# Filler matmuls ahead of an output projection, two equal evictions, and an early sqrt table in a one-core decode kernel

## The chip, the cores and the metric

The kernel runs on one core of one Trainium2 chip. The metric is the device time of one execution in microseconds; lower is better. Executions agree to a few tenths of a microsecond, so 2% (3.7 us) is far outside the noise. Where a profile is read, times are counted from the start of its span, which is about 1.3 us shorter than the time of the run. In the views PE is TensorE (matrix multiplication), PEld its loading of the stationary operand, ACT is ScalarE, DVE VectorE, POOL GpSimd, and SP is SyncE, whose queue issues the loads. The granted clock is the share of its full speed at which TensorE was allowed to run.

## The reference, cut to what matters

One decode step of an adaptive-LayerNorm block: two rows of 640 numbers, 32 heads of 192, a window of 1024 cached keys and values per head, a gated feed-forward part of 1536 hidden units.

```python
mod = (_silu(c) @ w_mod).reshape(c.shape[0], 6, 1, -1)      # sa, ca, ga, sb, cb, gb
h = _layernorm(x) * (1 + ca) + sa
# A: attention over the last 1024 cached positions, then @ wo   (6144 x 640)
x = x + ga * A(h)
h = _layernorm(x) * (1 + cb) + sb                            # "LN2"
# B: (gelu(h @ w_gate) * (h @ w_up)) @ w_down                  (640 x 1536, 1536 x 640)
x = x + gb * B(h)
```

With two rows there is hardly any arithmetic per byte: 76.9 MB of weights and cache are read once for one small result. The weights are loaded in this order, in one queue: w_mod, wq, the cache tiles, wo (two parts), w_gate, w_up, w_down (three parts).

## The kernel before

After attention, everything hangs on one chain: `sel` (gathers the attention result), wo, the row sums of wo, the residual, LN2, gate, up, the product, its transposition, down, the residual, the store. The parts that the change touches:

```python
S.op("pe", p_sel, ...)                                        # sel
S.op("act", ... activation(out=oT, in_=ps[:, BK_OT, ...], func=Copy), name="oT")
NA = D - QW                                                   # 640 = 512 + 128
for ci, (t0, n) in enumerate(WO_SPLIT):                       # 39 tiles, then 9
    ...
    for bk, lo, w in ((2, 0, QW), (3, QW, NA)):               # one matmul of 512, one of 128
        last = e.matmul(ps[32*i:32*i+B, bk, 0:w], lhsT=oT[:, t, :], rhs=wv[:, tl, lo:lo+w],
                        ..., tile_position=(0, 32*i))         # i = t % 4: four column strips
S.op("act", ... activation(out=wS[:, 0:QW], in_=ps[:, 2, :], func=Copy), name="wo_evac0")
S.op("dve", ... tensor_copy(out=wS[:, QW:D], in_=ps[:, 3, 0:NA]), name="wo_evac1")
# [cut: row sums, residual]
def ln_stats(tag):
    ...                                                       # act: Square with row sum; dve: sum; pe: both
    S.op("dve", ... tensor_copy(out=mv, in_=ps[:, BK_M, CS:CS+2]))           # mean, mean of squares
    S.op("dve", ... nvar = mean*mean - meansq)
    S.op("dve", ... nvar = -nvar + EPS)
    S.op("act", ... activation(out=st2[:, 0:1], in_=nvar, func=Sqrt))        # a table load stands in front
    S.op("dve", ... reciprocal(out=rstd, in_=st2[:, 0:1]))
def ln_mod(...):
    S.op("dve", ... lnt = (X - mean) * (1 + scale))
    S.op("dve", ... hrow = lnt * rstd + shift)
# [cut: transposition of hrow to h2T]
def ffn_gu(...):                                              # gate, then up
    wk = wv[:, k, :].rearrange("p (m i r) -> p i m r", i=NR, r=FR)   # strip i reads 3 of every 12 elements
    for i in range(NR):
        e.matmul(ps[32*i:32*i+B, bk, 0:FT], lhsT=h2T[:, k, :], rhs=wk[:, i, :, :], tile_position=(0, 32*i))
```

## Time and profile before

| | |
|---|---|
| time, median of the first 3 runs | 186.26 us (186.07 to 186.29) |
| span of the profiled run | 184.8 us |
| DMA busy, mean of 16 engines | 97% in the load queue |
| read from memory | 76.88 MB, 416 GB/s over the span |
| granted TensorE clock, mean | 0.878 |

From the page of the kernel before: three of the rows that cut the span into 40 slices (granted clock and DMA share in tenths), and the line on memory. The clock falls in several places. The DMA share stays at 7 tenths or more in every slice but the last.

```profile
PEclk9999999999999669997569999978999559975858
DMA  9999998999798989999898989999998989899980
...
HBM read 76.88 MB, written 0.00 MB: 416 GB/s over the span
```

The chain of work that ended last, in order of time (start us, us, what), of the kernel before, cut to the pieces that matter. After wo has landed at 164.57 it waits for no DMA: it runs through wo (6.31), a table load (1.28), gate and up (3.66), down (1.04).

```profile
137.63 26.94 DMA arena<-in_A_wo_dram
...
164.61 6.31 PE ps L629 x96
...
173.29 1.28 ACT L421
...
174.58 0.21 ACT st L421
...
176.38 3.66 PE ps L663 x34
...
181.28 1.04 PE ps L691 x48
```

The windows of the kernel before (stretch, its length, busy time of PE, PEld, DVE, ACT and POOL with instruction counts, granted clock, DMA share, GB/s). In the first stretch PE is busy for 1.38 of 3.40 us; in the two after it, which hold wo, the clock is at 0.50.

```profile
160.20:163.60 3.40, 1.38 (x20) 0.71 (x14) 0.19 (x1) 0.86 (x2) 0.00 (x0) 1.00 0.88 367
163.60:167.00 3.40, 2.39 (x36) 0.67 (x20) 0.00 (x0) 0.00 (x0) 0.00 (x0) 0.50 1.02 433
167.00:170.40 3.40, 3.40 (x56) 0.93 (x28) 0.00 (x0) 0.00 (x0) 0.00 (x0) 0.50 1.01 428
```

Last, the load stream beside that chain. First the loads' issue times on SyncE's queue (timeline), then the list of DMA issues (KB each, us from issue to landing), both of the kernel before.

```profile
155.90 0.33 SPq L285 DMA_DIRECT2D arena<-in_B_w_up_dram  x1
156.27 1.40 SPq L285 DMA_DIRECT2D arena<-in_B_w_down_dram  x3
```

```profile
arena<-in_B_w_up_dram SPq DMA_DIRECT2D x1, 1920.0 KB, 21.3
...
arena<-in_B_w_down_dram SPq DMA_DIRECT2D x1, 1280.0 KB, 24.0
arena<-in_B_w_down_dram SPq DMA_DIRECT2D x1, 480.0 KB, 24.7
arena<-in_B_w_down_dram SPq DMA_DIRECT2D x1, 160.0 KB, 24.6
```

Issue plus time to landing gives 177.2 us for w_up and 180.3, about 181.5 and 181.9 for the parts of w_down (the three issues lie about 0.47 us apart).

### The profile page before, as it was taken

Reading aid. Unit: us, or ns where it says so; the run is one execution under the profiler, and the core shown is the slowest. Engines: PE = TensorE matmul, PEld = TensorE weight load, DVE = VectorE, ACT = ScalarE, POOL = GpSimd, SP = SyncE. Lnnn points to the kernel's source line nnn. Section 1 sums busy time; section 2 is a strip of 40 time slices with the busy share of each in tenths; the row PEclk is TensorE's granted clock in tenths of the full one; section 3 lists DMA queues with packets and bytes.
Section 4 is the critical chain, followed back from the end, with each engine's and each line's share of the span. In section 5 each row is a group of like instructions: output and inputs, shape, how many; then the busy total and the mean of one; then the engine's idle time right before and its main releaser. Section 6 shows DMA issues by size and latency. Waiting matters only on the chain.

```text
span 184.8 us, 1589 instructions
## 1 busy us (share of the span) xinstructions
PE 104.6 (57%) x826; PEld 28.5 (15%) x549; DVE 106.7 (58%) x99; ACT 14.5 (8%) x27; POOL 6.5 (4%) x27
## 2 busy tenths in 40 slices
PE   0016300956665095653599565947663299849182
PEld 0012000120000000002360001600000256512042
DVE  6214000039994499964992999587995547600502
ACT  2032100041000000001000000010000100100720
POOL 7600000000000000000000000000000000000000
PEclk9999999999999669997569999978999559975858
DMA  9999998999798989999898989999998989899980
GB/s 333 466 479 426 426 426 362 440 426 505 346 511 362 489 383 468 457 394 502 351 493 351 500 362 489 404 447 426 436 482 362 502 357 508 357 395 432 422 361 26
DMA packets 2626, 76.97 MB, mean 417 GB/s; under 512 B 314, under 2 KB 444, under 8 KB 572
## 3 DMA queue, kind: packets, MB, share of 16 engines
q1 hardware_dynamic: 2604, 76.88, 97.0%
q8 instruction: 5, 0.08, 0.2%
q14 instruction: 1, 0.01, 0.0%
q10 hardware_dynamic: 16, 0.01, 0.0%
HBM read 76.88 MB, written 0.00 MB: 416 GB/s over the span
## 4 chain that ended last, share of the span: by engine, by line
DMA 57%; DVE 20%; PE 19%; ACT 2%; issue 1%; DVEq 0%
DMA arena<-in_A_k_cache_dram 35%; DMA arena<-in_A_wo_dram 15%; DVE arena L506 11%; DMA arena<-in_w_mod_dram 7%; PE ps L518 5%; DVE S_sb L525 4%; PE ps L569 4%; PE ps L629 3%; PE ps L458 2%; PE ps L663 2%; DVE Em L555 1%; ACT L421 1%; PE ps L691 1%; DVE hrow L430 0%; PE ps L439 0%
## 5 line engine op out<-in xcount | busy, mean ns | idle before, releaser
L518 PE MATMUL ps<-arena,ident_b 128*128 128x512 bf16 x192 | 49.1, 399 | 29.0 <-DVE arena L506 29.0
L506 DVE TENSOR_TENSOR arena<-arena,qbc 128x3072 bf16<-128x3072 bf16 x32 | 54.8, 1753 | 9.8 <-DMA arena<-in_A_k_cache_dram 9.8
L569 PE MATMUL ps<-arena,Em 128*64 128x384 bf16 x256 | 26.9, 381 | 5.6 <-DVE Em L555 5.6
L525 DVE TENSOR_REDUCE S_sb<-ps 128x32 f32<-128x1024 f32 x16 | 19.5, 1222 | 8.2 <-PE ps L518 8.2
L569 PEld LDWEIGHTS ps<-arena,Em 128*64 128x64 bf16 x256 | 16.6, 129 | 31.0 <-DVE Em L555 22.0
L555 DVE TENSOR_TENSOR Em<-E_sb,maskE 128x2048 bf16<-128x2048 bf16 x8 | 18.0, 2285 | 3.8 <-PE ps L569 3.8
L480 PE MATMUL ps<-arena,hT 128*2 128x512 bf16 x60 | 6.0, 587 | 11.8 <-DMA arena<-in_A_wq_dram 11.8
L490 DVE CAST qrow<-ps 128x512 bf16<-128x512 f32 x1 | 0.7, 692 | 17.0 <-PE ps L480 17.0
L533 PEld LDWEIGHTS ps<-ident_f,M 128*1 128x1 f32 x2 | 0.2, 79 | 60.9 <-DVE M L531 60.9
L629 PE MATMUL ps<-arena,oT 128*2 128x512 bf16 (+1 forms) x96 | 6.3, 454 | 2.4 <-DMA arena<-in_A_wo_dram 2.4
L637 DVE COPY arena<-ps 128x128 f32<-128x128 f32 x1 | 0.3, 293 | 10.6 <-PE ps L629 10.6
L543 ACT ACTIVATE E_sb<-S_sb,nbias 128x256 bf16<-128x256 f32 x2 | 1.0, 507 | 67.0 <-DVE nbias L541 67.0
L576 ACT ACTIVATE On<-ps,rden 128x384 bf16<-128x384 f32 x2 | 1.2, 580 | 49.9 <-PE ps L569 49.9
L399 PE MATMUL ps<-ident_b,crow 2*128 2x2 bf16 x5 | 0.4, 177 | 7.9 <-DMA crow<-in_c_dram 7.9
L458 PE MATMUL ps<-arena,scT 128*17 128x480 bf16 x40 | 4.3, 597 | 0.3 <-DMA arena<-in_w_mod_dram 0.3
L412 PE MATMUL ps<-st,selstat 128*128 128x2 f32 x4 | 0.9, 298 | 6.1 <-ACT sqj L408 6.1
L404 DVE CAST X<-xr 128x160 f32<-128x160 bf16 x1 | 0.2, 243 | 6.4 <-DMA xr<-in_A_x_dram 6.4
L663 PE MATMUL ps<-arena,h2T 128*2 128x384 bf16 x40 | 3.6, 507 | 0.3 <-DVE h2T L443 0.3
L480 PEld LDWEIGHTS ps<-arena,hT 128*2 128x2 bf16 x20 | 0.7, 118 | 16.8 <-issue 16.8
L466 DVE TENSOR_SCALAR opc<-modR 128x160 f32<-128x160 f32 x2 | 0.5, 244 | 4.3 <-ACT modR L463 4.3
L439 PE MATMUL ps<-selrow,hrow 128*32 128x2 bf16 x40 | 0.7, 182 | 3.8 <-DVE hrow L430 3.8
L672 DVE TENSOR_TENSOR aR<-ps,gl 128x384 bf16<-128x384 f32 x1 | 0.6, 557 | 3.8 <-PE ps L663 3.8
(84 smaller groups left out, 52.7 us busy)
## 6 DMA issues: line engine op xcount, KB each, us to landing
arena<-in_A_v_cache_dram SPq DMA_DIRECT2D x4, 6144.0 KB, 26.7
arena<-in_A_k_cache_dram SPq DMA_DIRECT2D x3, 6144.0 KB, 36.9
arena<-in_A_wq_dram SPq DMA_DIRECT2D x1, 7680.0 KB, 31.1
arena<-in_A_wo_dram SPq DMA_DIRECT2D x1, 6240.0 KB, 26.9
arena<-in_A_k_cache_dram SPq DMA_DIRECT2D x2, 3072.0 KB, 42.9
arena<-in_w_mod_dram SPq DMA_DIRECT2D x1, 4800.0 KB, 13.8
arena<-in_B_w_gate_dram SPq DMA_DIRECT2D x1, 1920.0 KB, 19.5
arena<-in_B_w_up_dram SPq DMA_DIRECT2D x1, 1920.0 KB, 21.3
```

Of the source, the lines that this page charges most:

```text
L421: S.op("act", lambda e: e.activation(out=st2[:, 0:1], in_=nvar[:, :], func=ACTF.Sqrt), reads=["nvar"], writes=[("st2", 0)], name=tag + "_s ...
L458: last = e.matmul(ps[32 * i:32 * i + RM, half, 0:MH].rearrange("p (m n) -> p m n", n=DR), lhsT=scT[:, k, :], rhs=wv[:, 3 * half:3 * half + ...
L480: last = e.matmul(ps[32 * i:32 * i + B, n, :], lhsT=hT[:, k, :], rhs=wv[:, kk, i, n * QW:(n + 1) * QW], start=(k == 0), stop=(k == KT - 1) ...
L506: S.op("dve", lambda e: e.tensor_tensor(out=kt, in0=kt, in1=qbc[:, b, :].unsqueeze(1).broadcast_to([P, JC, Dh]), op=ALU.mult), reads=[("qb ...
L518: last = e.matmul(o_ap, lhsT=ident_b[:, :], rhs=kt[:, :, t * GC:(t + 1) * GC], start=(t == 0), stop=(t == NCH - 1))
L525: S.op("dve", lambda e: e.tensor_reduce(out=S_sb[:, b, 2 * JC * pair:2 * JC * (pair + 1)], in_=ps[:, 2 * z:2 * z + 2, :].rearrange("p k (j ...
L555: S.op("dve", lambda e, z=z, j=j: e.tensor_tensor(out=Em[:, z, :, :], in0=E_sb[:, b, j:j + JE].unsqueeze(2).broadcast_to([P, JE, H]), in1= ...
L569: last = e.matmul(ps[64 * i:64 * i + 2 * H, BK_O, 0:ON], lhsT=Em[:, z, 2 * jp:2 * jp + 2, :].rearrange("p j h -> p (j h)"), rhs=view(it, l ...
L576: S.op("act", lambda e: e.activation(out=On[:, b, :], in_=ps[:, BK_O, 0:ON], func=ACTF.Identity, scale=rden[:, b:b + 1]), reads=[bank(BK_O ...
L629: last = e.matmul(ps[32 * i:32 * i + B, bk, 0:w], lhsT=oT[:, t, :], rhs=wv[:, tl, lo:lo + w], start=(t < NR), stop=(t >= NT - NR), tile_po ...
L663: last = e.matmul(ps[32 * i:32 * i + B, bk, 0:FT].rearrange("p (m r) -> p m r", r=FR), lhsT=h2T[:, k, :], rhs=wk[:, i, :, :], start=(k == ...
L691: last = e.matmul(ps[32 * i:32 * i + RM, BK_OT, CY:CY + DR], lhsT=aT[:, fc, :], rhs=wv[:, i, :], start=(fc == WD_SPLIT[0][0]), stop=(fc == ...
```

## The change

Its intent is to shorten the chain after attention: keep PE busy while it waits for wo, so that wo, which ran at a granted clock of 0.50 before, runs at full clock (`clock0`), and again around LN2 (`clock1`, `clock2`); evict wo's sums in two halves of equal length; load the sqrt table while PE waits for wo; drop the separate variance operation by adding EPS where the mean is copied and letting sqrt scale by -1; and compute the scaled difference while sqrt runs.

```diff
+        def keep_clock(n, name):      # n matmuls of 128x512, result never read
+            ... e.matmul(ps[:, BK_T, :], lhsT=ident_b, rhs=Em[:, 0, ...], start=True, stop=True)
         def ln_stats(tag):
+            if tag == "ln2":
+                keep_clock(5, "clock2")
-            S.op("dve", ... tensor_copy(out=mv, in_=ps[:, BK_M, CS:CS + 2]))
+            S.op("dve", ... tensor_tensor(out=mv, in0=ps[:, BK_M, CS:CS + 2], in1=epsc, op=add))
-            S.op("dve", ... tensor_scalar(out=nvar, in0=nvar, scalar1=-1.0, scalar2=EPS, ...))
-            S.op("act", ... activation(out=st2[:, 0:1], in_=nvar, func=Sqrt))
-            S.op("dve", ... reciprocal(out=rstd, in_=st2[:, 0:1]))
+            S.op("act", ... activation(out=st2[:, 0:1], in_=nvar, func=Sqrt, scale=-1.0))
         def ln_mod(...):
             S.op("dve", ... lnt = (X - mean) * (1 + scale))
+            S.op("dve", ... reciprocal(out=rstd, in_=st2[:, 0:1]))
 [cut]
         S.op("pe", p_sel, ...)
+        keep_clock(9, "clock0")
         S.op("act", ... name="oT")
+        S.op("act", ... activation(out=junk, in_=epsc[:, 0:1], func=Sqrt), name="sqrt_table")
-        NA = D - QW
+        NA = D // 2
-                    for bk, lo, w in ((2, 0, QW), (3, QW, NA)):
+                    for bk, lo, w in ((2, 0, NA), (3, NA, NA)):
 [cut: wo_evac0 and wo_evac1 with NA columns each]
         S.op("pe", wo_rows, ...)
+        keep_clock(5, "clock1")
```

## The prediction

> **What bounds the kernel now.** The page gives the DMA queues 97% of 16 engines over the span of 184.8 us, at 416 GB/s; the weight stream never pauses. The list of DMA issues, with its time to landing, puts the last arrivals (estimates: issue plus time to landing) at: first part of wo 164.6 us, second part 168.0, w_gate 172.6, w_up 177.2, the three parts of w_down 180.3, 181.5 and 181.9. The chain of waits says instead that the tail is compute: from wo's landing at 164.57 it runs through wo, LN2, gate/up, down without waiting for DMA. Both are nearly true: down's 48 matmuls run 181.28 to 182.32, and the last of them need bytes that land at 181.9. So the compute chain has only about 0.1 to 0.3 us over the DMA stream.
>
> **What the change does, step by step.**
> - Fillers. The windows show the granted clock falling to 0.50 at 163.6 us, so all of wo (6.27 us, groups of eight matmuls every 0.53 us) ran at half clock.[...] Nine 512-column fillers (about 0.22 us each warm, 0.43 cold: estimates from half and full-clock columns of wo) fit in the 2.36 us for which PE waits for wo. At full clock wo0 would end about 167.2, then wait for the second part (168.0) and end about 168.7 instead of 170.92: 2.2 us.
> - Halves. The ScalarE eviction of 512 columns took 0.60 us; 320 should take about 0.45 on each engine. 0.15 us.
> - Sqrt. The table load took 1.28 us[...] and held sqrt until 174.58, when its input had been ready at 174.41. With one small DVE operation gone (0.15) and the scaled difference (0.37 busy) behind the sqrt, 0.7 to 0.8 us.
> - The later fillers (five each) fit into PE idle of 1.3 us if warm; if cold they cost up to 0.8 us.
>
> Added up: 3 us of chain, h2T at about 173.2 instead of 176.34. Then the DMA takes it back. Gate may start at 173.2, but up cannot start before w_up lands at 177.2; it was at 178.3 before. The intermediate is ready about 179.5, down0 waits until 180.3, down1 until 181.5, the last four matmuls until 181.9. They take 0.24 us warm[...]; down ends near 182.15 to 182.25 against 182.32. The last 2.5 us (two DVE operations and the store) are unchanged. The diff moves no large load, and their issues all hang on earlier stages.
>
> **Predicted time.** 186.1 us (before: 186.26), range 185.6 to 186.5. Faster by over 2%: 1%; within 2%: 98%; slower: 1%.
>
> **What would show it.** wo's group spacing 0.27 us, no idle before wo beyond the landing, PE then waiting for the second part of wo; only one table load between wo and gelu; new waits of up and down on the DMA of w_up and w_down; the chain ending in DMA of w_down; last landings unmoved within 0.2 us.
>
> **What would make it wrong.** If the last landings move: the tail of the stream is uneven[...]. Or if the fillers run cold and late enough to use up the 3 us of slack, which I doubt.

That fillers keep the clock up was then the author's assumption; with them wo ran at 1.00 in the profile after. 2.2, 0.15 and 0.7 to 0.8 us come to the 3 us. One figure behind down's end is cut, the time of its last four matmuls at the lower clock. With the 0.24 us (down's matmuls took 233 ns on average in the profile before) 181.9 gives about 182.15; the way up to 182.25 is allowance. That the end of the stream is uneven shows in the profile before: the DMA share drops from 9 to 4 tenths at about 179.5 us and stays at 2 or 3 tenths until about 181.3.

## The result, and the profile after

| | before | after |
|---|---|---|
| time, median (6 runs each) | 186.05 us (185.89 to 186.29) | 185.97 us (185.91 to 186.12) |
| ratio | | 0.9996, 95% interval 0.9983 to 1.0009 |
| span of the profiled run | 184.8 us | 184.9 us |
| mean granted clock, profiled run | 0.878 | 0.926 |

A ratio is the mean time of one kernel's runs over that of the other's of the same rounds, so it is not quite the ratio of the medians quoted. The result is "same": nothing that the noise lets one see.

The slices of the profile after: the clock is full from the 34th slice on. The DMA row looks as before.

```profile
PEclk9999999996999759998599999987999669999999
```

The timeline of the profile after (start us, us, engine, line, operation; in brackets the idle time before and what ended it):

```profile
161.13 1.89 PE L415 MATMUL ps<-Em,ident_b 128*128 128x512 bf16 x8
161.41 1.28 ACT L632 ACT_TABLE_LOAD   x1
...
164.80 2.89 PE L643 MATMUL ps<-arena,oT 128*2 128x320 bf16 x78 [1.78 <-DMA arena<-in_A_wo_dram]
...
168.27 0.98 PE L643 MATMUL ps<-arena,oT 128*2 128x320 bf16 x18 [0.58 <-DMA arena<-in_A_wo_dram]
...
172.58 0.20 ACT L433 ACTIVATE st<-nvar 128x1 f32<-128x1 f32 x1 [0.98 <-DVE nvar L430]
...
174.09 1.91 PE L678 MATMUL ps<-arena,h2T 128*2 128x384 bf16 x20 [0.27 <-DVE h2T L455]
...
177.45 1.91 PE L678 MATMUL ps<-arena,h2T 128*2 128x384 bf16 x20 [1.45 <-DMA arena<-in_B_w_up_dram]
...
181.70 0.64 PE L706 MATMUL ps<-arena,aT 128*17 128x160 bf16 x16 [0.31 <-DMA arena<-in_B_w_down_dram]
182.09 0.10 PEld L706 LDWEIGHTS ps<-arena,aT 128*17 128x17 bf16 x4 [0.21 <-DMA arena<-in_B_w_down_dram]
```

The fillers ahead of wo and the LN2 part did what they were meant to. wo ran at full clock, waited for its second part, and was done at 169.25 in place of 170.92. Sqrt started at 172.58 in place of 174.58. Gate started at 174.09 in place of 176.38, 2.3 us earlier. Then the new waits begin: up stands 1.45 us until w_up has landed, and both later parts of down wait for w_down. Down ended where it had ended before (182.37, before 182.32). The chain of the profile after says it shortest: it no longer holds wo or LN2 but reaches from w_down's load to the end.

```profile
155.58 26.07 DMA arena<-in_B_w_down_dram
181.65 0.04 issue
181.70 0.39 PE ps L706 x12
182.08 0.01 issue
182.09 0.28 PE ps L706 x4
182.37 0.02 issue
182.39 0.34 DVE fin L711
```

### The profile page after: what moved, and what is told of

It reads as the page before. It is cut to its first block, busy times and chain, and to the rows that moved or that the text cites. A ratio compares the mean times of both kernels' runs of the same rounds, so it can differ in the third digit from the quotient of the medians.

```text
span 184.9 us, 1610 instructions
## 1 busy us (share of the span) xinstructions
PE 104.3 (56%) x843; PEld 26.1 (14%) x552; DVE 106.8 (58%) x97; ACT 14.5 (8%) x28; POOL 6.7 (4%) x29
## 4 chain that ended last, share of the span: by engine, by line
DMA 57%; DVE 22%; PE 17%; ACT 1%; issue 1%; SPq 0%
DMA arena<-in_A_k_cache_dram 36%; DMA arena<-in_B_w_down_dram 14%; DVE arena L518 12%; DMA arena<-in_w_mod_dram 8%; PE ps L581 8%; DVE S_sb L537 6%; PE ps L530 5%; DVE Em L567 2%; PE ps L470 2%; DVE negm L547 1%; ACT E_sb L555 1%; PE ps L558 1%; DVE M L543 0%; PE ps L551 0%; SPq L287 0%
## 5 line engine op out<-in xcount | busy, mean ns | idle before, releaser
L530 PE MATMUL ps<-arena,ident_b 128*128 128x512 bf16 x192 | 50.7, 411 | 30.2 <-DVE arena L518 30.1
L581 PE MATMUL ps<-arena,Em 128*64 128x384 bf16 x256 | 24.5, 357 | 5.6 <-DVE Em L567 5.6
L581 PEld LDWEIGHTS ps<-arena,Em 128*64 128x64 bf16 x256 | 15.4, 121 | 29.8 <-DVE Em L567 22.2
L492 PE MATMUL ps<-arena,hT 128*2 128x512 bf16 x60 | 4.7, 485 | 11.7 <-DMA arena<-in_A_wq_dram 11.7
L651 DVE COPY arena<-ps 128x320 f32<-128x320 f32 x1 | 0.5, 491 | 10.1 <-PE ps L643 10.1
L643 PE MATMUL ps<-arena,oT 128*2 128x320 bf16 x96 | 3.9, 299 | 2.4 <-DMA arena<-in_A_wo_dram 2.4
L415 PE MATMUL ps<-Em,ident_b 128*128 128x512 bf16 x17 | 4.2, 379 | 0.2 <-issue 0.2
```

Source lines behind the costliest of these rows:

```text
L415: last = e.matmul(ps[:, BK_T, :], lhsT=ident_b[:, :], rhs=Em[:, 0, 0:512 // H, :].rearrange("p j h -> p (j h)"), start=True, stop=True)
L492: last = e.matmul(ps[32 * i:32 * i + B, n, :], lhsT=hT[:, k, :], rhs=wv[:, kk, i, n * QW:(n + 1) * QW], start=(k == 0), stop=(k == KT - 1) ...
L530: last = e.matmul(o_ap, lhsT=ident_b[:, :], rhs=kt[:, :, t * GC:(t + 1) * GC], start=(t == 0), stop=(t == NCH - 1))
L581: last = e.matmul(ps[64 * i:64 * i + 2 * H, BK_O, 0:ON], lhsT=Em[:, z, 2 * jp:2 * jp + 2, :].rearrange("p j h -> p (j h)"), rhs=view(it, l ...
L643: last = e.matmul(ps[32 * i:32 * i + B, bk, 0:w], lhsT=oT[:, t, :], rhs=wv[:, tl, lo:lo + w], start=(t < NR), stop=(t >= NT - NR), tile_po ...
```

## The experiments

**Theory.** The stream of loads ends at the same time in both kernels, and its end bounds both; the chain got about 2 us shorter and now waits. **Rivals**: (A) the stream alone matters and the chain was far from it in both kernels; (B) the chain never got shorter in sum, since the fillers and the table load cost what they gave. Twelve kernels were run, each in 5 rounds on one of three chips; the kernel before ran beside them, with medians of 186.00, 186.02 and 185.99 us. To see the chain at all one has to take the end of the stream away, so most of them load only one fifth of w_up, which makes w_down land about 3.7 us earlier (an estimate; its middle part landed at 177.9 us in place of 181.65). Their outputs are wrong, which doesn't matter for the times. The instructions on the compute engines stay the same.

### 1. The end of the stream taken away, kernel before

```diff
-    S.dma("sp", k_dma(view(it), source(it)), ...)
+    cut = F if it[0] == "wu" else place[it][1]           # w_up: 1536 of 7680 elements per partition
+    S.dma("sp", k_dma(view(it, 0, cut), source(it)[:, 0:cut] ...), ...)
```

> The kernel before, with only one fifth of w_up loaded (wrong result on purpose), so that everything loaded after it lands about 3.7 us earlier (1.57 MB at 416 GB/s). Theory (two nearly equal bounds: compute chain just ahead of the DMA stream in the kernel before): no gain, 0 to 0.3 us, because the compute chain from wo on stays. Rival A (the DMA stream alone bounds both kernels): 3 us or more faster. Rival B (the change never shortened the chain): no gain here and none in the changed kernel either.

Measured: median 185.12 us (184.63 to 185.88, 6 runs) against 186.00, ratio 0.9951 (0.9933 to 0.9970). This is 0.9 us, more than the 0 to 0.3 expected, and far less than rival A's 3 us. The six runs spread over 1.25 us, where the kernel before spread over 0.4. So in most runs the compute chain of the kernel before was already shorter than the stream, by up to 1.4 us, and the end of the stream hid how much it varied. The one profile that I had read, of a run at 186.16 us, was a long one. Its wo ran 6.31 us; in the profile of this experiment wo took 5.65: the step between its groups of eight matmuls fell from 0.53 to 0.27 us at about 169 us, where in the profile before the granted clock rose from 0.50 to 1.00 only at 170.4.

```profile
164.67 5.65 PE ps L631 x96
...
180.67 1.04 PE ps L693 x48
```

### 2. The same for the changed kernel

The edit is that of experiment 1, in the changed kernel.

> The changed kernel with the same cut load (wrong result on purpose). Theory: with up no longer waiting for w_up the chain shows its true gain: down ends about 2.1 us earlier than in the changed kernel, so about 183.8 to 184.0 us, 2.0 to 2.3 us under the kernel before. Rival A (DMA alone): 3 us or more faster, as much as the kernel before gains from the same cut. Rival B (the change's fillers and loads cost what they gave): about 186.0, no gain.

Measured: median 183.61 us (183.50 to 183.79, 4 runs), ratio 0.9870 (0.9857 to 0.9883). This is a little under the expected 183.8 to 184.0. Both rivals fall: the chain is shorter by 1.5 us between the medians of the two cut kernels (185.12 and 183.61), yet the gain is not what a stream alone would give. In its chain down starts at 178.87, in place of 180.67 above, without a wait for w_down.

```profile
173.94 3.69 PE ps L680 x22
...
178.87 1.04 PE ps L708 x48
```

### 3. The stream made longer, both kernels

Here 393 KB more are loaded between w_up and w_down into a free part of the arena; nobody reads them and the results are right.

```diff
+    place[("pad", 0)] = (o_d + FC * D, 13 * HS - o_d - FC * D)     # 1536 elements per partition
 [cut]
+    if kind == "pad":
+        return B_w_up.rearrange("(p k) n -> p (k n)", k=KT)[:, 0:place[it][1]]
```

> The kernel before with 393 KB more to load between w_up and w_down (0.95 us of stream at 416 GB/s; nobody reads it, the result stays right). Theory: the stream had about 0.1 to 0.25 us to spare, so 0.7 to 0.9 us slower. Rival B, compute alone: under 0.2 us slower.

> The changed kernel with the same 393 KB more to load. Theory: it already waits for the last bytes of w_down, so the whole 0.95 us shows (0.85 to 1.05 us slower than the changed kernel), about 186.95. Rival B, compute alone: under 0.2 us slower.

Measured: before 186.94 us (186.87 to 187.03), ratio 1.0049 (1.0037 to 1.0061); after 187.00 (186.92 to 187.09), ratio 1.0052 to the kernel before (1.0040 to 1.0064). The changed kernel lost 1.03 us (187.00 against its 185.97 of other rounds), as expected. The kernel before lost 0.94, a shade more than the 0.7 to 0.9 expected: it loses all of the 0.95 us, so it too waits for the stream in most runs. Together with experiment 1 this settles what bounds the two kernels. In the profile of the kernel before with the longer stream, down waits for w_down where it did not before:

```profile
181.43 0.73 PE L694 MATMUL ps<-arena,aT 128*17 128x160 bf16 x32 [0.56 <-DMA arena<-in_B_w_down_dram]
```

### 4. Which part of the change shortened the chain

Four kernels with the cut load, each with one part of the change taken out. The edits: all three `keep_clock` calls removed; only `clock1` and `clock2` removed; `NA = D - QW` and its evictions put back; the LN2 operations put back and `sqrt_table` removed.

> Changed kernel, cut w_up load, without any filler matmuls (halves and sqrt part kept). Theory (fillers give the wo stage, and what they give depends on where the run's 3.4 us clock windows fall): 0.9 to 1.8 us slower than the changed kernel with the cut load (183.61), so 184.5 to 185.4, and the runs spread by about 1 us again as those of the kernel before with the cut load did (184.63 to 185.88), not by 0.3. Rival C (fillers are worth nothing, gain is sqrt alone): within 0.2 us of 183.6.

> Changed kernel, cut w_up load, with the nine fillers ahead of wo alone, the five and five around LN2 taken out. Theory (gate and up ran at 0.35 us a group at full clock as at half, so the clock there is worth nothing): within 0.15 us of 183.61. Rival D (later fillers keep gate and up fast): 0.5 us or more slower.

> Changed kernel, cut w_up load, wo sums split 512/128 as before. Trace: from the end of wo to the start of its row sums 0.67 us in the kernel before, 0.66 in the changed one. Theory from that: within 0.1 us of 183.61. My recorded prediction gave this step 0.15 us.

> Changed kernel, cut w_up load, LN2 as before (table load in front of sqrt, separate variance operation, scaled difference after the sqrt). Trace: from the statistics matmul to the start of the last LN2 operation 1.89 us before, 1.28 changed. Theory: 0.6 us slower than 183.61, about 184.2. My recorded prediction gave this step 0.7 to 0.8.

| cut load, changed kernel | median us | range | ratio to before |
|---|---|---|---|
| whole change | 183.61 | 183.50 to 183.79 | 0.9870 |
| no fillers | 184.98 | 184.29 to 185.52 | 0.9941 |
| only the nine ahead of wo | 183.65 | 183.36 to 184.53 | 0.9866 |
| halves undone | 183.79 | 183.61 to 184.50 | 0.9888 |
| LN2 part undone | 184.68 | 184.04 to 185.26 | 0.9928 |

All fillers together are worth 1.4 us between medians, as expected (the nine ahead of wo alone 1.3: 184.98 against 183.65), and without them the spread of 1.2 us is back. The ten later ones are worth 0.04. The halves are worth 0.2 between medians, more than the 0.1 expected. But the profiled run of that kernel, its slowest at 184.50, shows another cause: the nine fillers ended at 162.64, PE then stood for 2.1 us, and wo ran at half clock for a time (5.11 us). Timeline and windows of that profile:

```profile
160.53 2.11 PE L417 MATMUL ps<-Em,ident_b 128*128 128x512 bf16 x9
164.76 5.11 PE L645 MATMUL ps<-arena,oT 128*2 128x512 bf16 x96 [2.12 <-DMA arena<-in_A_wo_dram]
170.58 0.47 PE L659 MATMUL ps<-arena,selw 128*17 128x160 f32 x8 [0.71 <-ACT arena L651]
...
172.41 0.35 PE L426 MATMUL ps<-st,selstat 128*128 128x2 f32 x2 [0.17 <-ACT sqj L422]
...
174.12 0.37 PE L453 MATMUL ps<-selrow,hrow 128*32 128x2 bf16 x20 [0.26 <-DVE hrow L444]
```

```profile
161.80:165.20 3.40, 1.28 (x16) 0.19 (x8) 0.00 (x0) 0.71 (x2) 0.00 (x0) 0.99 0.92 385
165.20:168.60 3.40, 3.40 (x58) 1.02 (x28) 0.00 (x0) 0.00 (x0) 0.00 (x0) 0.50 1.03 438
```

The same 5.11 us of wo stand in the profiled runs of the kernels with nine fillers alone (its slowest, 184.53) and with the LN2 part undone (its slowest, 185.26). So the nine fillers hold the clock in some runs and not in others. This goes with where the clock's windows of 3.41 us happen to lie: in the profile of the changed kernel the window from 161.27 still held 1.75 us of busy PE and the clock stayed full; in the fence above the window held 1.28 and it fell (a count over two traces stands below, under "Fillers ahead of wo"). From the end of wo to the row sums PE waits as long without halves as with them: 0.71 us here, 0.67 in the profile after. The three best runs without halves (183.61 to 183.79) lie inside the range of the whole change. I take the halves as worth nothing that these runs can show.

The LN2 part cost 1.07 us between medians where 0.6 was expected; that number too mixes in runs with a fallen clock. The traces compare better, since the profiled runs of these two kernels have the same clock history: from the statistics matmul to LN2's transposition it is 174.12 - 172.41 = 1.71 us above, and 174.91 - 172.58 = 2.33 us with LN2 as before. That is 0.62 us. Timeline of the kernel with the LN2 part undone:

```profile
172.58 0.35 PE L426 MATMUL ps<-st,selstat 128*128 128x2 f32 x2 [0.16 <-ACT sqj L422]
...
174.91 0.25 PE L455 MATMUL ps<-selrow,hrow 128*32 128x2 bf16 x8 [0.87 <-DVE hrow L446]
```

### 5. Why gate and up did not profit from the clock

In the profile before, gate and up took 3.66 us at half clock (granted 0.50). In the changed kernel with the cut load they took 3.69 at full clock (1.00). A rival reading is that something beside the reading of the weights, such as the weight loads of the array, holds them. In the first two kernels here, strip i reads 384 neighbouring elements in place of 3 out of every 12 (a step of 24 bytes); the third is the first without `clock1` and `clock2`.

```diff
-    wk = wv[:, k, :].rearrange("p (m i r) -> p i m r", i=NR, r=FR)
+    wk = wv[:, k, :].rearrange("p (i m r) -> p i m r", i=NR, r=FR)   # another order of hidden units
```

> Changed kernel, cut w_up load, and gate and up read each weight row as four runs of 384 neighbouring elements in place of groups of 3 elements 24 bytes apart (another order of the hidden units, so a second wrong result on purpose). Theory (the 24-byte step, not the clock, sets two of the four column strips to 0.35 us a group): at full clock a group takes 0.16 us, gate and up together 2.1 us in place of 3.66, down then starts near the cut stream's end (last landing about 178.3), so 1.2 to 1.5 us under 183.61. Rival E (something else in these matmuls, such as weight loads, holds them): within 0.3 us of 183.61.

> Kernel before, cut w_up load, same neighbouring reads. Theory: at half clock a group takes 0.32 us with either reading, and no filler keeps the clock up, so 0 to 0.5 us under the 185.12 of the cut kernel before, much less than in the changed kernel.

> As cut_contig but without the ten fillers around LN2. Theory: now that gate and up can use the clock, these fillers are worth something, 0.3 to 1.2 us on average, with runs spread by their clock phase; with the strided reading they were worth 0.1.

Measured: changed kernel 182.48 us (182.38 to 182.70), ratio 0.9812, 1.1 us under 183.61; kernel before 184.65 (184.08 to 186.50), ratio 0.9943, 0.5 us under 185.12 and with a wide spread; changed without the later fillers 183.38 (183.22 to 184.12), ratio 0.9867, so these fillers are now worth at least 0.9 us where they were worth 0.04. The answers on gate's and up's line in the changed kernels (min/median/max duration of the 40 matmuls in ns, first and last start in us), first with the strided reading, then with the neighbouring one:

```profile
L680 PE MATMUL ps<-arena,h2T x40: 391/456/532, 173.9 to 177.1; 128*2 128x384 bf16 x40
```

```profile
L680 PE MATMUL ps<-arena,h2T x40: 323/326/326, 173.9 to 175.3; 128*2 128x384 bf16 x40
```

Then, of the kernel with neighbouring reads, the timeline of the same matmuls, and the pieces of its chain that follow:

```profile
173.85 1.80 PE L680 MATMUL ps<-arena,h2T 128*2 128x384 bf16 x40 [0.28 <-DVE h2T L457]
```

```profile
156.29 21.56 DMA arena<-in_B_w_down_dram
177.85 0.04 issue
177.89 0.66 PE ps L708 x16
```

Gate and up fell from 3.66 us busy to 1.80 at the same clock; rival E falls. Two sizes of the expectation were off: gate and up took 1.80 us and not 2.1, and the 1.1 us gained lie just under the 1.2 to 1.5 expected. In the profile of the kernel before with neighbouring reads they took 3.17 us, and in that of the changed kernel without the later fillers 3.37, so now the fillers count. The granted clock over these matmuls was not read in these two profiles; that it was half for most of them is an estimate from the 1.80 us at full clock. Of the expected 0.32 us a group at half clock "with either reading" the profile before shows the strided one, for two of the four strips (0.32 us; the other two took 0.35); for neighbouring reads it was an estimate. The chain in the last fence ends in w_down's load again: with this the chain caught up even with the shortened stream, which is why 1.1 us showed and not all of 1.9.

### 6. More fillers ahead of wo

`keep_clock(9, "clock0")` becomes 13, with the cut load.

> Changed kernel, cut w_up load, 13 fillers ahead of wo in place of nine. In the profiles of the runs at 184.5 us the nine fillers ended at 162.6 us and PE stood idle for 2.1 us till wo landed; the clock then fell at 165 and wo ran at half speed up to 168.5. Theory: with 13 the idle is at most 1.3 us, no run has wo at half clock, all runs within 183.4 to 183.9. Rival F (number of fillers doesn't matter): one or two runs of five or six at 184.2 to 184.6 as in the three ablations before.

Measured: 183.66 us (183.57 to 183.72, 4 runs), ratio 0.9873. No slow run, but the nine fillers of experiment 2 showed none in four either, and this profiled run came with a late `sel`. So the experiment does not tell the theory from rival F. What its timeline does show is that too many fillers cost nothing here: they ended at 165.08, 0.45 us after wo's landing (estimate from the issue: 164.6), and wo's first part, starting at 165.00, still had to wait for its second.

```profile
162.11 2.97 PE L417 MATMUL ps<-Em,ident_b 128*128 128x512 bf16 x13
165.00 2.89 PE L645 MATMUL ps<-arena,oT 128*2 128x320 bf16 x78
168.12 0.98 PE L645 MATMUL ps<-arena,oT 128*2 128x320 bf16 x18 [0.23 <-DMA arena<-in_A_wo_dram]
```

## Why the prediction was right

The prediction was 186.1 us (185.6 to 186.5); measured were 185.97. Its main step, "then the DMA takes it back", is shown: new waits of up and down on their loads, a chain that ends in w_down's load, and experiments 1 to 3, in which the two kernels part by 1.5 us as soon as the load stream ends earlier and lose about as much as was added when it ends later (0.94 and 1.03 us). The forecast gain over the kernel before was too small to be told from none. Added up, the chain was to be 3 us shorter at the start of gate; it was 2.3 us (174.09 in place of 176.38). Point by point:

- **What bounds the kernel.** Put as "the compute chain has only about 0.1 to 0.3 us over the DMA stream". That held for the profiled run and not for most others. Experiments 1 and 3 show that the kernel before, too, usually waits for the stream. The free chain of its runs varies by 1.25 us, with the place at which the clock rises inside wo as the visible cause in two profiles. One profile is one draw of the clock.
- **Fillers ahead of wo**, predicted 2.2 us. wo ended 1.67 us earlier (169.25). The term that was too small is the second part: it took 0.98 us after its landing at 168.2 where I had left 0.6 to 0.7 after a landing at 168.0, since nine tiles on four strips are three rounds and not two and a quarter (in the profile after the rounds start 0.27 us apart, the third, of a single tile, at 168.81). Over many runs these nine are worth 1.3 us (183.65 against 184.98). As to the clock: in the profiles before and after its changes lie multiples of 3.41 us apart. Counted in these two traces, over the windows of 3.41 us from 37.3 us on before and from 35.0 on after: a full clock fell to half after all 12 windows with PE busy for 1.41 us or less, and stayed after all 53 with 1.47 or more; a half clock rose after all 11 with 2.67 or more and after none of the 10 with 2.40 or less. This is a count only: no run set the share on purpose, some matmul records can be missing, and the figures are those of two profiles, not limits. Above, a gap of 2.1 us went with a fall, after a window with PE busy for 1.28 of 3.40 us; in the kernel before the fall came after one with 1.38 of 3.40.
- **Halves**, predicted 0.15 us. The ACT eviction did fall from 0.60 to 0.44 us, but DVE's rose from 0.29 to 0.49, and the row sums then began about 0.14 us after it in place of 0.05. Next to nothing is left.
- **LN2**, predicted 0.7 to 0.8 us, measured 0.62. In the profiles before and after, 0.32 us of it lie between the statistics matmul and the start of sqrt (1.16 before, 0.84 after), and of these the table load can explain only the 0.17 for which it held a sqrt whose input was ready; 0.29 lie behind sqrt, where the scaled difference had been counted with 0.37. The table load took 1.28 us in both kernels and moved out of the chain. In the profile before it adjoined its neighbours: ScalarE's operation ahead of it ended at 173.28, the load ran from 173.29 for 1.28 us, and sqrt started at 174.58.
- **Later fillers**, feared to cost up to 0.8 us. They cost nothing and gave nothing, because the matmuls after them read with a 24-byte step. For the same reason up took 1.91 us at full clock, the transposed product came at 180.58 where I had put it at 179.5, and the wait of down's first part (landed at 180.5) did not come. The runs give the size: the 40 matmuls took 3.66 us with 6-byte pieces 24 bytes apart and 1.80 us with neighbouring elements, both at a granted clock of 1.00. In the profile after, too at full clock, the strips differ: on column strips 0 and 3 a matmul of gate started every 0.23 us, on strips 1 and 2 every 0.35. Why strips 1 and 2 are the slower ones was not shown; no run changed the place of the pieces alone.
- **Landings unmoved within 0.2 us.** w_down's middle part landed at 181.65 by the chain, against an estimate of 181.5 before. By the semaphore updates in the two traces everything from wo on landed 0.16 to 0.21 us later after: wo 164.76 against 164.57, w_up 177.41 against 177.21, the last part of w_down 182.05 against 181.88.

What stays open: why the last loads land just where they do, as the single DMA engines were not told apart; and from exactly which share of busy PE on the clock is kept, which the count above only brackets. No version that beats both kernels came out of this, since the experiments point to the stream, and the change does not touch it.

## What to carry to other kernels

Before shortening a chain of compute, write the landing time of each of its loads beside it; a gain counts only up to the next load that it would have to wait for. To measure such a change anyway, shorten the stream behind it and compare both kernels there. And check that what a faster clock should speed up is bound by the clock at all: two runs of the same matmuls at half and at full clock tell (here the strided ones took 3.66 us at 0.50 and 3.69 at 1.00).
